# Query products of the late head pairs as 64x64 tiles in two banks

## Chip, cores and metric

The kernel runs on one core of a Trainium2 chip. The metric is the device time of one execution in microseconds (us), median of the runs. Engines: TensorE (PE; its weight loads are PEld), VectorE (DVE), ScalarE (ACT), GpSimd (POOL), and SyncE (SP), which issues most DMAs.

## What is computed

Linear attention with a norm, followed by a gated layer with spatial mixing:

```python
# batch 8, heads 8, seq 576, head_dim 64
kv  = einsum('bhsd,bhse->bhde', k, v)
out = einsum('bhsd,bhde->bhse', q, kv)
rms = sqrt(mean(out * out, axis=-1, keepdims=True) + 1e-06)
x   = (out / rms * g_norm)            # then to (batch, seq, 512)

h = maximum(x @ w_in, 0)              # 512 -> 1024
u, v = h[..., :512], h[..., 512:]
v_n = (v - mean(v)) / sqrt(var(v) + 1e-06)
v_s = einsum('ts,bsd->btd', w_spatial, v_n) + b_spatial[None, :, None]
result = (u * v_s) @ w_out            # 512 -> 512
```

## The kernel before

Heads are taken in pairs: pair p of batch b holds heads 2p and 2p+1, so a pair has 128 rows of head dimension. The sequence of 576 is four chunks of 128 and a tail of 64 rows, which is handled apart (`tail_a`, `tail_b`, `att_tail`). The large stages (`hv`, the u products, the spatial products, `out_unit`) split each f32 value into a high and a low fp32r part and use three products.

For batches 2 to 7 the attention of a batch is computed during the gated layer of the batch before. `att_four` (L172) forms the key-value products of all four pairs in two banks, copies their diagonal 64x64 blocks into `KVB` (a block for each pair, off-diagonal blocks zero), and then calls `att_two` (L207), which forms the query products of pairs 0 and 1 as 64x64 tiles: 32 calls, four to a slot of 64 rows by head and by half chunk, head 0 into one bank, head 1 into the other. Its matmuls are recorded on L181, those of a helper that queues each one behind the first. A call with f32 operands runs as two matmul instructions. `two_norm` (L219) takes the norm of one bank, that is of one head of both pairs: ScalarE squares the bank at once, VectorE sums it, `rsqrt` (ScalarE L272, VectorE L277 to L279) gives the factor, and VectorE multiplies it into one half of the columns of both `X2[0]` and `X2[1]`, strided.

Pairs 2 and 3 go through `att_q` one after the other: `att_qa` (L309) issues four 128x128 matmul calls against the whole block of `KVB` (L313) into one bank, then `norm_a` squares the bank in eight blocks of 64 with ScalarE's accumulator (L296), and `norm_b` (L305) multiplies the factor in. The result is one of `X2[0]` and `X2[1]`, in turn. `att_t` (L341) transposes a pair's result into a bank, and `split_x` (L334 ScalarE, L335 VectorE) writes the high and low part into `XH` and `XL`. All attention banks come from `ps_att`, three buffers in rotation.

The steps of a batch are put in a list by `att_steps` and are called where a letter `s` stands in the strings `FIRST`, `EVEN` and `ODD` (L53 to L66), between the products (`u`, `p`, `o`) of the running batch. For odd batches the late steps (T0, T1, Q2, Q3, T2, T3, then a copy of the tail) begin two products into the spatial stage (`p`); seven of its 14 products stand before Q2, one between Q3 and T2. For even batches three products stand before Q2, and five between Q2 and T2. The program order is a priority: the order on each engine is made when the program is built, from what is expected to be ready; `issue_after` alone keeps an instruction behind another on its engine. After each query product `issue` queues loads on SyncE: a query buffer is loaded again when its product has read it (`qt`, two buffers).

Of the kernel before, what the change touches and what calls it, by code (L numbers as in the profile page):

```python
# [8 lines left out]
F32 = mybir.dt.float32  # L9
# [3 lines left out]
AF = mybir.ActivationFunctionType  # L13
ALU = mybir.AluOpType
AX = mybir.AxisListType

B, H, S, D = 8, 8, 576, 64
DM, FF = 512, 1024
FH = FF // 2
P = 128  # L20
# [53 lines left out]
def body(ctx: ExitStack, tc, qT, kvm, kvt, g2, w_in, wsT, bsp, w_out, out):  # L74
    nc = tc.nc
# [11 lines left out]
    def persistent(shape, dt, name):  # L87
        return const.tile(shape, dt, name=name, tag=name)
# [29 lines left out]
    KVB = persistent([P, NP, P], F32, "KVB")  # L118
# [4 lines left out]
    ident = persistent([P, P], F32, "ident")  # L123
    gcol = persistent([P, 16], F32, "gcol")[:, 0:1]
    SUM = {n: persistent([P, 2, HS], F32, f"SUM{n}") for n in ("p1", "u2", "u3", "g")}
    n_gate, n_x, X2 = [0], [0], []
    edge = ctx.enter_context(tc.tile_pool(name="edge", bufs=1, side="right"))
    epsc = edge.tile([P, 8], F32, name="epsc", tag="epsc")[:, 0:1]

# [3 lines left out]
    keys, queries = {}, {}  # L133
# [70 lines left out]
        issue()  # L204
        issue()

    def att_two(b, st, matmul):  # L207

        qts = [queries.pop((b, i)) for i in range(2)]
        st["two"] = [ps_att.tile([P, 512], F32, name="pso", tag="att") for _ in range(2)]  # L210
        for c in range(NC):
            for j in range(2):
                for half in (0, D):
                    for h in (0, D):
                        at, t = (j * NC + c) * D, c * P + half
                        matmul(st["two"][h // D][half:half + D, at:at + D], qts[j][h:h + D, t:t + D],
                               st[j][h:h + D, h:h + D], start=True, stop=True)

    def two_norm(st, h):  # L219
        ps = st["two"][h]  # L220
        x = X2[2].rearrange("p j (c g e) -> p (j c) g e", g=2, e=D)[:, :, h]
        ss = small.tile([P, 8], F32, name="ss", tag="ss")
        nc.scalar.activation(x, heads(ps), AF.Square)
        nc.vector.tensor_reduce(ss, x, axis=AX.X, op=ALU.add)
        r = rsqrt(ss, 8, P, 1.0 / D, "h")
        nc.vector.tensor_tensor(x, heads(ps), r.unsqueeze(2).broadcast_to([P, 8, D]), op=ALU.mult)
        st[h] = X2[h]

    def att_k(b, pairs, st, copy=nc.vector.tensor_copy):
        ps = ps_att.tile([P, 512], F32, name="pskv", tag="att")  # L230
        to = KVB
        ends, first = [], None

        def product(p, of, h, c):
            at = (p - pairs[0]) * P + h
            return nc.tensor.matmul(ps[h:h + D, at:at + D], of[:, 0, h:h + D], of[:, 1, h:h + D],  # L236
                                    start=c == 0, stop=c == NC)

        for p in reversed(pairs):
            kv, kt, qs = keys.pop((b, p))  # L240
            for c in range(NC + 1):
                of = kv[:, :, c] if c < NC else kt
                for h in (0, D):
                    if first is None:
                        first = product(p, of, h, c).ins
                    else:
                        with tc.high_priority(), tc.issue_after(first):
                            product(p, of, h, c)
            st[p] = to[:, p]
            ends.append((p, qs))  # L250
        both = ps[:, 0:len(pairs) * P].rearrange("p (j e) -> p j e", e=P)
        own = slice(p, p + len(pairs))
        copy(to[0:D, own, 0:D], both[0:D, :, 0:D])
        nc.scalar.copy(to[D:P, own, D:P], both[D:P, :, D:P])  # L254
        for p, qs in reversed(ends):
            if qs is not None:
                att_end(p, st, qs)
        issue()
# [7 lines left out]
    def rsqrt(ss, n, rows, mul, tag):  # L266

        return rsqrt_b(*rsqrt_a(ss, n, rows, mul, tag))

    def rsqrt_a(ss, n, rows, mul, tag):  # L270
        y, r = (small.tile([P, n], F32, name=f"{x}{tag}", tag=f"{x}{tag}")[0:rows] for x in "yr")
        nc.scalar.activation(y, ss, AF.Abs_reciprocal_sqrt, bias=epsc[0:rows], scale=mul)  # L272
        return ss, y, r, mul
# [8 lines left out]
    def heads(ap):  # L282
        return ap.rearrange("p (h e) -> p h e", e=D)

    def norm_a(ps, rows=P, accumulate=False, soon=False):
        n = ps.shape[1] // D
        if soon:
            x = work.tile([P, 512], F32, name="xt", tag="stg", bufs=2)[:, 0:n * D]
        else:
            x = (X2[n_x[0] % 2] if X2 else pool_x.tile([P, 512], F32, name="x", tag="x"))[0:rows, 0:n * D]  # L290
            n_x[0] += 1
        ss = small.tile([P, 8], F32, name="ss", tag="ss")[0:rows, 0:n]
        if accumulate:
            for h in range(n):
                cols = slice(h * D, (h + 1) * D)
                nc.scalar.activation(x[:, cols], ps[0:rows, cols], AF.Square,  # L296
                                     accum_out=ss[:, h:h + 1])
        else:
            nc.scalar.activation(x, ps[0:rows], AF.Square)
            nc.vector.tensor_reduce(ss, heads(x), axis=AX.X, op=ALU.add)  # L300
        return ps, x, rows, rsqrt_a(ss, n, rows, 1.0 / D, "h")
# [21 lines left out]
    def att_q(b, p, st):  # L323
        att_qa(b, p, st, b > 1 and True)
        att_qb(b, p, st)

    def tail_a(b, st, accumulate=False, soon=False):
        st["xt"] = norm_a(st["tail"], P, accumulate, soon)

    def tail_b(b, st):  # L330
        st["xt"] = norm_b(*st["xt"])
# [5 lines left out]
    def att_t(b, p, st):  # L337
        x = st[p]
        ps = ps_att.tile([P, 512], F32, name="pstr", tag="att")
        for c in range(NC):  # L340
            nc.tensor.transpose(ps[:, c * P:(c + 1) * P], x[:, c * P:(c + 1) * P], ident)  # L341
        hi, lo = (X0H, X0L) if b == 0 else (XH, XL)
        split_x(ps, hi[:, p, 0:NT], lo[:, p, 0:NT])

    def att_tail(b, st):
        x = st["xt"]
        ps = ps_att.tile([P, 512], F32, name="pstt", tag="att")
        for p in range(NP if b < 2 else 2):
            nc.tensor.transpose(ps[:, p * P:(p + 1) * P], x[:, p * P:(p + 1) * P], ident)
        cols = slice(TAILC[b % 2], TAILC[b % 2] + TAIL)  # L350
        hi, lo = (X0H, X0L) if b < 2 else (XH, XL)
        n, i = (P, P - TAIL) if b < 2 else (TAIL, 0)
        v = ps[:, 0:NP * n].rearrange("q (p t) -> q p t", t=n)[:, :, i:n]
        split_x(v, hi[:, :, cols], lo[:, :, cols])
        if b == 1:
            own = slice(TAILC[0], TAILC[0] + TAIL)
            for to, of in (XH, hi), (XL, lo):
                nc.gpsimd.dma_start(f32(to[:, :, own]), f32(of[:, :, cols]))
# [7 lines left out]
    def att_steps(b):  # L366

        st = states.setdefault(b, {})

        def t2():  # L370
            att_t(b, 2, st)
            tail_a(b, st)
            tail_b(b, st)

        def tail():
            tail_a(b, st)
            tail_b(b, st)

        K = [lambda p=p: att_k(b, (p, p + 1), st) for p in (0, 2)]
        Q = [lambda p=p: att_q(b, p, st) for p in range(NP)]  # L380
        T = [lambda p=p: att_t(b, p, st) for p in range(NP)]
        end = lambda: att_tail(b, st)
        if b > 1:
            N = [lambda h=h: two_norm(st, h) for h in range(2)]
            late = [T[0], T[1], Q[2], Q[3], T[2], T[3]]
            if b % 2 == 0:
                return [*[K[0], lambda: att_four(b, st)] * (b == 2), *N, *late[:4], t2, T[3], end], []
            return [*N, lambda: (tail_a(b, st, soon=True), tail_b(b, st)), end], [*late, move_tail]
        if b % 2 == 0:
            return [*K[:1], Q[0], Q[1], T[0], *K[1:], Q[2], T[1], Q[3], t2, T[3], end], []  # L390
        return K + [tail, end], [Q[0], Q[1], T[0], Q[2], T[1], Q[3], T[2], T[3], move_tail]
# [360 lines left out]
    pool_x = opening.enter_context(tc.tile_pool(name="x", bufs=2))  # L752
# [120 lines left out]
    def room(b, p, kind):  # L873
        if kind == "q":
            return sum((x == 0) <= (y < 2) for x, y in queries) < 2
        return in_u(b, p) or sum(not in_u(*x) for x in keys) < 2

    def issue():

        while wanted[0] and todo and room(*todo[0]):  # L880
            wanted[0] -= 1
            att_load(*todo.pop(0))
# [47 lines left out]
    def enqueue(b, late=0):  # L930
        if b < NB:
            queue.extend(att_steps(b)[late])
# [55 lines left out]
    st = [states.setdefault(b, {}) for b in range(2)]  # L988
# [135 lines left out]
```

## Time and profile before

| | us |
|---|---|
| span of the profiled execution | 491.9 |
| three timed runs | 492.62, 495.11, 495.78 |
| their median | 495.11 |
| TensorE busy, VectorE busy, ScalarE busy | 482.5, 383.5, 276.4 |

The span goes from the first to the last instruction of the one profiled execution; the time of that execution beyond its span isn't listed, and the runs are 0.7 to 3.9 us above it. Busy times are shares of the span. In a timeline a row is one or more like instructions in a run, with the start of the first, and the time to the end of the last; as matmuls overlap, a row's slot is the time to the start of the next row.

### The profile page before, as it was taken

To read this page: it belongs to the slowest core of one execution; us is meant where nothing else is said; L and a number is where in the kernel's file an instruction comes from. 1 tells how busy PE (TensorE), PEld (TensorE's weight loads), DVE (VectorE), ACT (ScalarE), POOL (GpSimd) and SP (SyncE) were. 2 spreads that over 40 slices of the span, in tenths; PEclk is the share of its full clock that TensorE was granted. 3 is DMA by queue.
4 is the path that set the end of the run, shared out by engine and by line. 5 is a ranking of instruction groups with operands and counts; after the bars stand their busy time and mean duration, and the time that the engine had idled before them with its cause. 6 is when DMAs were issued, how large, how long until landed. Compare 5 with 4: busy or idle time off the path is not lost.

```text
span 491.9 us, 10170 instructions
## 1 busy us (share of the span) xinstructions
PE 482.5 (98%) x3796; PEld 434.9 (88%) x3796; DVE 383.5 (78%) x1029; ACT 276.4 (56%) x818; POOL 35.9 (7%) x71
## 2 busy tenths in 40 slices
PE   6999999999999999999999999999999999999996
PEld 6879999998978899889997899979998889989995
DVE  1889997884986797877986798977887779877770
ACT  3799845876425783368424694257733678246322
POOL 5001100000121010010000000010000101010000
PEclk9999999999999999999999999999999999999999
DMA  8999333553377036471536426372324702333413
GB/s 258 365 278 328 78 113 115 179 178 121 97 262 227 27 82 261 138 228 45 190 126 189 151 68 218 116 209 100 104 113 139 225 1 61 144 94 121 135 39 107
DMA packets 30357, 74.13 MB, mean 151 GB/s; under 512 B 6786, under 2 KB 9858, under 8 KB 28772
## 3 DMA queue, kind: packets, MB, share of 16 engines
q1 hardware_dynamic: 24852, 47.61, 30.1%
q0 software_dynamic: 5456, 25.87, 16.0%
q8 instruction: 30, 0.49, 0.4%
q14 instruction: 19, 0.16, 0.1%
HBM read 58.09 MB, written 13.11 MB: 145 GB/s over the span
## 4 chain that ended last, share of the span: by engine, by line
PE 90%; DMA 3%; DVE 3%; ACT 1%; SPq 1%; issue 0%; DVEq 0%
PE pso L398 21%; PE psh L431 17%; PE psb L638 7%; PE psub L638 6%; PE psa L638 6%; PE psc L638 5%; PE psuc L638 4%; PE psua L638 4%; PE pso L313 4%; PE pskv L181 3%; PE psu L398 3%; PE pstr L341 3%; PE psh L398 2%; DMA stage<-w_out 2%; PE pso L181 1%; PE pskv L236 1%
## 5 line engine op out<-in xcount | busy, mean ns | idle before, releaser
L398 PE MATMUL pso<-WO,G 128*128 128x512 f32 x384 | 95.6, 395 | 0.0
L398 PEld LDWEIGHTS pso<-WO,G 128*128 128x128 f32 x384 | 70.5, 188 | 15.2 <-issue 0.9
L434 ACT CAST G<-SUMg 128x288 fp32r<-128x288 f32 (+1 forms) x56 | 22.2, 405 | 62.0 <-DVE SUMg L660 62.0
L740 ACT COPY o<-pso 128x512 f32<-128x512 f32 x35 | 19.8, 588 | 52.8 <-PE pso L398 44.4
L435 DVE TENSOR_TENSOR VL<-v,VH 128x512 fp32r<-128x512 f32 (+1 forms) x60 | 36.4, 615 | 11.0 <-ACT VH L434 10.6
L431 PE MATMUL psh<-WVH,XH 128*128 128x512 f32 x112 | 43.8, 391 | 0.0
L431 PE MATMUL psh<-WVH,XL 128*128 128x512 f32 x112 | 43.7, 391 | 0.0
L431 PE MATMUL psh<-WVL,XH 128*128 128x512 f32 x112 | 43.6, 389 | 0.0
L434 ACT CAST VH<-v 128x512 fp32r<-128x512 f32 (+1 forms) x60 | 32.8, 563 | 11.6 <-DVE v L463 10.9
L418 ACT ACTIVATE v<-v,mv,rv 128x512 f32<-128x512 f32 x28 | 22.8, 813 | 7.8 <-DVE mv L417 6.1
L410 DVE BATCH_NORM_STATS2 s<-v 128x6 f32<-128x512 f32 x32 | 22.1, 692 | 5.4 <-ACT v L404 4.8
L431 PEld LDWEIGHTS psh<-WVH,XL 128*128 128x128 f32 x112 | 21.0, 188 | 4.6
L638 PE MATMUL psb<-WSH,VH 128*128 128x288 f32 x84 | 25.1, 300 | 0.0
L435 DVE TENSOR_TENSOR G<-SUMg,G 128x288 fp32r<-128x288 f32 (+1 forms) x56 | 23.4, 420 | 2.1
L431 PEld LDWEIGHTS psh<-WVL,XH 128*128 128x128 f32 x112 | 21.0, 188 | 4.4
L431 PEld LDWEIGHTS psh<-WVH,XH 128*128 128x128 f32 x112 | 21.0, 188 | 4.3
L638 PE MATMUL psb<-WSL,VH 128*128 128x288 f32 x84 | 24.7, 295 | 0.0
L638 PE MATMUL psb<-WSH,VL 128*128 128x288 f32 x84 | 24.1, 294 | 0.0
L404 ACT ACTIVATE v<-psh 128x512 f32<-128x512 f32 x32 | 19.1, 597 | 6.8 <-PE psh L431 5.8
L313 PE MATMUL pso<-KVB,qt 128*128 128x128 f32 x144 | 20.8, 293 | 1.8 <-DMA qt<-qT 1.3
L313 PEld LDWEIGHTS pso<-KVB,qt 128*128 128x128 f32 x144 | 19.5, 206 | 2.6 <-ACT KVB L254 2.2
L334 ACT ACTIVATE XH<-pstr,gcol 128x512 fp32r<-128x512 f32 x28 | 18.7, 688 | 5.3 <-PE pstr L341 5.3
(281 smaller groups left out, 1417.8 us busy)
## 6 DMA issues: line engine op xcount, KB each, us to landing
WO<-spare_o POOLq DMA_DIRECT2D x12, 1024.0 KB, 6.5
KV<-kvm SPq DMA_DIRECT2D x19, 512.0 KB, 5.5
UX<-spare_u POOLq DMA_DIRECT2D x18, 512.0 KB, 5.7
out<-o SPq DMA_DIRECT2D x32, 256.0 KB, 2.3
qt<-qT SPq DMA_DIRECT2D x28, 256.0 KB, 3.7
U<-kvm SPq DMA_DIRECT2D x12, 512.0 KB, 4.0
stage<-w_in SPq DMA_DIRECT2D x8, 512.0 KB, 7.5
KT<-kvt SPq DMA_DIRECT2D x32, 64.0 KB, 4.8
```

Of the source, the lines that this page charges most:

```text
L181: first[0] = nc.tensor.matmul(*args, **kw).ins
L313: nc.tensor.matmul(ps[:, c * P:(c + 1) * P], qt[:, c * P:(c + 1) * P], st[p], start=True, stop=True)
L334: nc.scalar.activation(hi, ps, AF.Copy, scale=gcol)
L398: nc.tensor.matmul(ps, lt, rh, start=i == 0, stop=i == n - 1)
L404: nc.scalar.activation(v, ps, AF.Relu)
L410: nc.vector.bn_stats(s6, v)
L418: nc.scalar.activation(v, v, AF.Identity, bias=m, scale=r)
L431: nc.tensor.matmul(ps, lt, rh, start=k == 0 and i == 0, stop=k == NP - 1 and i == 2)
L434: nc.scalar.copy(hi, x)
L435: nc.vector.tensor_tensor(lo, x, f32(hi), op=ALU.subtract)
L638: nc.tensor.matmul(ps, lt, rh, start=start and i == 0, stop=stop and i == len(pairs) - 1, skip_group_check=True)
L740: nc.scalar.copy(o, ps)
```

## The change

Pairs 2 and 3 of batches 2 to 7 go through `att_two` and `two_norm` as well. One step, `late_two`, issues 32 calls of 64x64 for both pairs, the first queued behind the last TensorE instruction traced, each further one behind the one before it, and then the two load steps; the norm of head 0 is part of that step, that of head 1 is the next. Their squares stay in blocks of 64 with ScalarE's accumulator. Each norm fills half of the columns of both `X2[0]` and `X2[1]`. The norm of an even batch's tail uses `X2[0]` as before.

```diff
-    n_gate, n_x, X2 = [0], [0], []
+    n_gate, X2 = [0], []
...
-    def att_two(b, st, matmul):
-
-        qts = [queries.pop((b, i)) for i in range(2)]
+    def att_two(b, st, matmul, first=0):
+
+        qts = [queries.pop((b, first + i)) for i in range(2)]
...
-                               st[j][h:h + D, h:h + D], start=True, stop=True)
-
-    def two_norm(st, h):
+                               KVB[h:h + D, first + j, h:h + D], start=True, stop=True)
+
+    def two_norm(st, h, first=0):
...
-        nc.scalar.activation(x, heads(ps), AF.Square)
-        nc.vector.tensor_reduce(ss, x, axis=AX.X, op=ALU.add)
+        if first:
+            for k in range(8):
+                nc.scalar.activation(x[:, k], ps[:, k * D:(k + 1) * D], AF.Square,
+                                     accum_out=ss[:, k:k + 1])
+        else:
+            nc.scalar.activation(x, heads(ps), AF.Square)
+            nc.vector.tensor_reduce(ss, x, axis=AX.X, op=ALU.add)
...
-        st[h] = X2[h]
+        st[first + h] = X2[h]
+
+    def last_pe():
+        return next(i for i in reversed(nc.cur_bb.bb.instructions) if i.engine == mybir.EngineType.PE)
+
+    def late_two(b, st):
+        row = [None]
+
+        def matmul(*args, **kw):
+            if row[0] is None:
+                with tc.issue_after(last_pe()):
+                    row[0] = nc.tensor.matmul(*args, **kw).ins
+                return
+            with tc.high_priority(), tc.issue_after(row[0]):
+                row[0] = nc.tensor.matmul(*args, **kw).ins
+
+        att_two(b, st, matmul, 2)
+        issue()
+        issue()
...
-            x = (X2[n_x[0] % 2] if X2 else pool_x.tile([P, 512], F32, name="x", tag="x"))[0:rows, 0:n * D]
-            n_x[0] += 1
+            x = (X2[0] if X2 else pool_x.tile([P, 512], F32, name="x", tag="x"))[0:rows, 0:n * D]
...
-            late = [T[0], T[1], Q[2], Q[3], T[2], T[3]]
+            late = [T[0], T[1], lambda: (late_two(b, st), two_norm(st, 0, 2)),
+                    lambda: two_norm(st, 1, 2), T[2], T[3]]
```

## Rows read from the trace of the kernel before

**Rows 1.** The page: span, and busy time of TensorE

```profile
span 491.9 us, 10170 instructions
...
PE 482.5 (98%) x3796; PEld 434.9 (88%) x3796; DVE 383.5 (78%) x1029; ACT 276.4 (56%) x818; POOL 35.9 (7%) x71
```

**Rows 2.** Waits of TensorE: us in total, times, longest us

```profile
PE pskv L236 <- DMA KV<-kvm: 1.7, 2, 1.4
PE pso L313 <- DMA qt<-qT: 1.3, 1, 1.3
...
```

**Rows 3.** The line of the late pairs' squares: duration min/median/max, first and last start

```profile
L296 ACT ACTIVATE xx<-pso x96: 201/250/376, 116.3 to 410.9; 128x64 f32<-128x64 f32 x96
```

**Rows 4.** Timeline of TensorE, batch 2, pairs 2 and 3 (start us, us)

```profile
115.17 1.06 PE L313 MATMUL pso<-KVB,qt 128*128 128x128 f32 x8
115.99 3.01 PE L398 MATMUL pso<-WO,G 128*128 128x512 f32 x12
118.83 1.06 PE L313 MATMUL pso<-KVB,qt 128*128 128x128 f32 x8
```

**Rows 5.** The same timeline: nine output matmuls among spatial ones

```profile
134.76 2.23 PE L398 MATMUL pso<-WO,G 128*128 128x512 f32 x9
136.83 0.29 PE L638 MATMUL psc<-WSH,VH 128*128 128x288 f32 x1
```

**Rows 6.** The same timeline: tiled products of batch 3, pairs 0 and 1

```profile
143.25 0.63 PE L398 MATMUL pso<-WO,G 128*128 128x512 f32 x2
143.81 0.69 PE L181 MATMUL pskv<-U 128*64 128x64 f32 x16
...
144.54 0.50 PE L398 MATMUL pso<-WO,G 128*128 128x512 f32 x1
144.88 1.76 PE L398 MATMUL pso<-WO,GT 128*128 128x512 f32 x7
...
148.23 1.16 PE L181 MATMUL pso<-KVB,qt 64*64 64x64 f32 x64
149.32 0.66 PE L181 MATMUL pst<-KVB,QS 128*64 128x128 f32 x8
```

**Rows 7.** Timeline of TensorE: end of batch 2's u products, transposes, spatial stage

```profile
176.20 0.95 PE L638 MATMUL psuc<-T,UX 128*128 128x288 f32 x6
176.99 0.96 PE L638 MATMUL psub<-T,UX 128*128 128x288 f32 x6
177.96 0.40 PE L638 MATMUL psub<-UX,WUH 128*128 128x288 f32 x1
178.20 0.29 PE L638 MATMUL psub<-T,WUH 128*128 128x288 f32 x1
...
179.65 0.60 PE L341 MATMUL pstr<-ident,xx 128*128 128x128 f32 x4
...
180.88 0.30 PE L638 MATMUL psa<-WSH,VH 128*128 128x288 f32 x1
```

**Rows 8.** Windows: length, then busy PE, PEld, DVE, ACT, POOL, clock, DMA

```profile
170.40:181.00 10.60, 10.59 (x82) 10.32 (x81) 9.62 (x35) 9.63 (x46) 1.07 (x2) 1.00 0.33 87
181.00:196.00 15.00, 15.00 (x144) 14.77 (x143) 12.11 (x31) 5.85 (x15) 1.11 (x2) 1.00 0.61 220
```

**Rows 9.** Timeline of ScalarE: first square and last read of batch 3's pair 2

```profile
171.52 0.22 ACT L296 ACTIVATE xx<-pso 128x64 f32<-128x64 f32 x1
...
173.01 0.25 ACT L296 ACTIVATION_READ_ACCUMULATOR xx<-pso 128x1 f32 x1
```

**Rows 10.** Timeline of SyncE: the two query loads after batch 3's late products

```profile
171.51 4.42 SPq L166 DMA_DIRECT2D qt<-qT  x2
```

**Rows 11.** The page, DMA issues: KB each, median us from issue to landing

```profile
qt<-qT SPq DMA_DIRECT2D x28, 256.0 KB, 3.7
```

**Rows 12.** Timeline of TensorE: batch 3's T0 and T1

```profile
159.74 1.04 PE L341 MATMUL pstr<-ident,xx 128*128 128x128 f32 x8
```

**Rows 13.** Timeline of VectorE: the scaled result of batch 3's pair 2

```profile
178.45 0.68 DVE L305 TENSOR_TENSOR xx<-pso,rh 128x512 f32<-128x512 f32 x1
```

## Prediction

> **What bounds the kernel now.** I read the page first, then who waited for whom on TensorE, then the timeline of TensorE around the touched products. The page [rows 1] has TensorE busy for 482.5 of 491.9 us. Busy can hide a wait, because pipelined matmuls overlap, so I looked at the waits: the two largest of TensorE are 1.7 and 1.3 us [rows 2] and concern loads of the opening. From the second batch on, TensorE issues one matmul behind another, and the time is the sum of their slots (start to next start), of the changes between kinds of matmul, and of little else. So the change is priced by the slots that it takes from TensorE and gives to it; what it does on the other engines counts only if TensorE comes to wait.
>
> **What is removed.** For pairs 2 and 3 of batches 2 to 7 there are 12 products; the squares of their norms stand as 96 blocks, 8 to a pair [rows 3]. Each product is four calls that run as 8 matmuls of 128x128. In batch 2 the first starts at 115.17 and what follows at 115.99, that is 0.82 us [rows 4]. The 12 matmuls that follow reach to 118.83, 2.84 us, where nine of that kind take 2.07 us elsewhere [rows 5], 0.230 each, or 2.76 for 12. So leaving the f32 product costs another 0.08. One pair costs 0.90 us, two cost 1.80 us a batch, six batches 10.8 us. Entering costs nothing that I can see.
>
> **What is added.** The trace already has the new form: pairs 0 and 1 of the same batches run as 64 matmuls of 64x64 into two banks, from 148.23 to 149.32, 1.09 us [rows 6]. This holds the work and the drains inside it. There the neighbours are other tiled products; the new block will stand among 128x128 ones, so an entry and an exit come on top. The nearest rows are the 20 tiled matmuls between output products: before them two matmuls take from 143.25 to 143.81, 0.56 where 0.46 is the pace, so the entry costs 0.10; behind them one takes 0.34 instead of 0.23, so the exit costs 0.11 [rows 5, 6]. The new block costs 1.09 + 0.10 + 0.11 = 1.30 us.
>
> **A rule weighed.** The rows put 0.21 us on the two changes of tiling, beside the drains already inside the 1.09 [rows 6]. The Trainium skill, TensorEngine Tiling, section Tiling Modes (Key Properties), says that a change of tiling mode, other than a change of tile, drains the engine; it gives no figure, and the trace agrees. Without any outer drain the gain would be 6 x (1.80 - 1.09) = 4.3 us, with them it is 6 x (1.80 - 1.30) = 3.0 us; I take the second.
>
> **The sum on TensorE.** 6 x 0.50 = 3.0 us less. Bounds: 4.3 us if each new block stands beside other f32 products, which then share the drains. On the other side, something may be placed inside the block: a visit of 128x128 matmuls costs an exit and an entry again, 0.21 outside, and about 0.15 inside (the 20 tiled matmuls take 0.73 where ten pairs at 0.058, an estimate from the pace inside that row, take 0.58), 0.36 together. One such cut in each batch leaves 6 x 0.14 = 0.8 us.
>
> **What moves.** The first of the new matmuls is queued behind the last TensorE instruction traced. In an odd batch's work this is the seventh product of the spatial stage, where the old products stood before that stage began (it begins at 180.88 [rows 7]; they ran from about 170 on). With it move 16 square blocks on ScalarE (count and width unchanged: 8 a pair before, 8 a bank now), two reciprocal roots, and eight VectorE instructions. They leave a stretch where VectorE is busy 9.62 and ScalarE 9.63 of 10.60 us for one with 12.11 and 5.85 of 15.00 [rows 8]. The moved work is about 3.5 us of ScalarE (two times 1.74, from 171.52 to the end of the last read at 173.26 [rows 9]) and some 2 us of VectorE, part of which lies in the second stretch already; both fit. I cost the move at nothing: TensorE's own products hide it. If that cover failed, the price is that of the third case below. The strided rather than contiguous writes of the squares and the scaled result cost nothing, as pairs 0 and 1 use the same layout now.
>
> Two query loads are also issued behind the block, together instead of one after each pair. Now they are issued from 171.51 on [rows 10] and land 3.7 us after issue [rows 11]. Behind the block in an odd batch there are still seven products of at least six matmuls at 0.13 and some 40 output matmuls at 0.23 before the next batch's early products read them, 5.5 + 9.2 = 14.7 us. Queued behind these loads on SyncE are the key loads of the next batch, wanted at the same late time. GpSimd's queue is not passed. So nothing is late there.
>
> The second of the two banks is the one that the first transpose (T0) filled; the old second product needed it as well, later than the first. T0 in batch 3 runs at 159.74 [rows 12], the new block after 180.88, so I cost this wait at nothing. If the block came too early, every instruction behind its second matmul would stand on TensorE until the split of T0 ends.
>
> One stall may go. In batch 3, six matmuls take 0.79 us (176.20 to 176.99), the next six 0.97, and one more 0.24 instead of 0.13 [rows 7], some 0.28 us in all, just where the second norm fills ScalarE and VectorE. If it comes from there it goes in three odd batches, 0.85 us; if not, nothing. I take nothing.
>
> **Rivals.** (a) Forecast: 3.0 us less by slots alone. The profiled span of 491.9 becomes 488.9. The median of the runs shown, 495.11, is 3.2 us above the profiled span (the lowest only 0.7 above), and I take the difference off the median: 492.1 us.
>
> (b) The block is cut up: other matmuls are placed between its first and its last. One cut in each batch leaves 0.8 us, 494.3 us; two make 6 x (0.50 - 0.72), 1.3 us slower, 496.4. For it: only order on TensorE is asked for, not closeness. Against: the 64 matmuls of pairs 0 and 1, traced the same way, stand in one piece [rows 6]. It is also the way in which the change does not do what it says.
>
> (c) Slower: the transposes of pair 2 wait. Before, T2 needed the norm of pair 2 alone, and T2 started 0.52 us after its result (178.45 + 0.68 = 179.13, T2 at 179.65 [rows 7, 13]). Now each head's norm fills half of both pairs, so T2 needs both norms: 2 x 1.74 of squares, 0.68 for the last product and about 0.8 for the small steps between (an estimate, from the three small and one root instruction that surround it), 5.0 us from the end of the block. In batches 3, 5 and 7 the program has just one product of the spatial stage in between, 8 x 0.13 = 1.1 us; if T2 keeps that place, TensorE stands 3.9 us in each, 11.8 us, and the time is 492.1 + 11.8 = 503.9 us. It decides against the change from 1.0 us of stall in each of these three batches. In batches 2, 4 and 6 there are over 5 us between. Against it: the order on TensorE is not that of the program: T0 of batch 3, which the program has behind two products of that stage, runs 21 us before them [rows 7, 12], so transposes are put where their operands are expected to be ready, and no wait of TensorE for a norm is among the largest [rows 2].
> The Trainium skill, TensorEngine Tiling, section Performance Considerations (PSUM Bottleneck), says that after such a speedup the emptying of PSUM may become what binds. By it this case would be the likely one; the rows so far show other work in that cover for pairs 0 and 1, and I give it the chance below.
>
> (d) Faster by more: the blocks share drains (4.3 us) and the stall of 0.28 us goes in three batches (0.85 us): 5.1 us, 490.0 us. For it: ScalarE and VectorE are relieved where both are over 90% busy [rows 8]. Against: all six blocks would have to find such neighbours.
>
> **How the numbers follow.** Chances: (a) 0.62, (b) 0.17, (c) 0.11, (d) 0.10. A measurement of this kernel tells about 1%, 5 us, from no change. (d) lies at that line and is counted as faster, and (a) comes out beyond it by its own scatter (the three runs span 3.2 us) with some 0.06: faster 0.16. (c) is slower: 0.11. The rest, 0.73, is within 1%. The range goes from 1.5 us under (d) to just over two cuts of (b), 488.5 to 497.0; (c) stays outside it.
>
> **What would show it.** Right: twelve pieces of 64 matmuls of 64x64 where there were six, each new one about 1.1 us with 0.1 more on either side; no product of 128x128 with KVB left after batch 1; waits of TensorE as small as now; the span 3 us shorter. A step is wrong if a new block starts late on a bank, if it is in several pieces, if T2 or T3 starts behind a wait for the second norm, or if the slots of the output and spatial products differ. The prediction falls if the span changes by under 1 or over 5 us.

## The result, and the profile after

The changed kernel takes 499.08 us (median of seven runs, 496.45 to 500.60) where the kernel before, in as many runs, takes 495.11 (492.62 to 496.20). The ratio is 1.0092 with a 95% interval from 1.0069 to 1.0115: 0.9% slower, some 4.5 us, where 3.0 us less were forecast; the time lies outside the range. Of the 6.0 us between the two profiled spans, 2.2 arose before 97 us, where both kernels run the same instructions in the same order. That opening varies from one execution to the next: its 701st matmul comes 96.1 us behind the first one after, 93.9 before, and 94.0 in the profiles of the first two experiments below. So 3.7 us remain to be explained.

The head of the page after, beside [rows 1]:

```profile
span 497.9 us, 10746 instructions
...
PE 480.0 (96%) x4084; PEld 430.3 (86%) x4084; DVE 384.3 (77%) x1029; ACT 276.2 (55%) x818; POOL 35.8 (7%) x71
```

TensorE is busy for 2.5 us less, which is nearly the 3.0 us that the slots promised. The span is longer all the same, so TensorE now waits. The waits of TensorE after, beside [rows 2] (us in total, times, longest us):

```profile
PE psub L661 <- DVE U L633: 3.3, 3, 1.1
PE psub L661 <- ACT v L427: 1.9, 2, 0.9
PE pso L335 <- DMA qt<-qT: 1.4, 1, 1.4
...
PE psub L661 <- ACT U L619: 0.6, 1, 0.6
```

The two at the head are new. They are u products (psua, psub and psuc are their banks, psa to psc those of the spatial stage), which the change doesn't touch: three wait for VectorE's addition to U, two for ScalarE's relu that empties a bank (L427). The one of 0.6 us, also new, is a u product of the last batch. The wait for a query load in the opening, 1.3 us before, is 1.4.

The new block itself, on TensorE's timeline after (batch 3, pairs 2 and 3; start us, us):

```profile
186.10 0.29 PE L669 MATMUL psa<-WTL,TB 128*128 128x288 f32 x1
186.32 0.27 PE L243 MATMUL pso<-KVB,qt 64*64 64x64 f32 x1
186.33 0.28 PE L246 MATMUL pso<-KVB,qt 64*64 64x64 f32 x3
186.43 0.22 PE L243 MATMUL pso<-KVB,qt 64*64 64x64 f32 x1
186.43 1.05 PE L246 MATMUL pso<-KVB,qt 64*64 64x64 f32 x59
187.41 0.40 PE L661 MATMUL psb<-WSH,VH 128*128 128x288 f32 x1
187.65 0.30 PE L661 MATMUL psb<-WSL,VH 128*128 128x288 f32 x1
```

All 64 matmuls stand in one piece, 1.09 us from 186.32 to 187.41. The slot ahead of them is 0.22 and that behind 0.24 where 0.13 is the pace, so 0.09 and 0.11 on top: 1.29 us, the 1.30 of the forecast.

What became of the time of the old products? In an odd batch's attention they stood in the u stage, at 170.43 and 174.51 in batch 3. After, the same stretch on TensorE:

```profile
175.61 1.75 PE L661 MATMUL psub<-T,UX 128*128 128x288 f32 x12
178.47 0.40 PE L661 MATMUL psub<-UX,WUH 128*128 128x288 f32 x1 [1.11 <-DVE U L633]
```

and on VectorE:

```profile
175.55 1.40 DVE L504 TENSOR_TENSOR TA<-v,TA 64x512 fp32r<-64x512 f32 x2
176.98 0.87 DVE L504 TENSOR_TENSOR TA<-SUMg,TA 64x256 fp32r<-64x256 f32 x2
177.88 0.16 DVE L300 SCALAR_TENSOR_TENSOR rv<-yv 128x1 f32<-128x1 f32 x1
177.96 0.81 DVE L633 TENSOR_TENSOR U<-psub,U 128x288 f32<-128x288 f32 x2
```

Twelve matmuls from 175.61 at 0.13 each are issued by 177.2. The product behind them goes on in the same bank, so it must wait until VectorE has read it (L633), and on VectorE the low part of the tail's v (L504, 2.3 us) stands ahead of that. Before, TensorE came to this place 0.18 us early [rows 7], with VectorE's addition (L610 there) at

```profile
177.46 0.45 DVE L610 TENSOR_TENSOR U<-psub,U 128x288 f32<-128x288 f32 x1
```

Counted from the start of the stage, that is 18.7 us before and 18.0 after: without the norms VectorE is 0.7 us sooner, but TensorE, without the two products, is 1.8 us sooner. So now it comes 1.3 us early.

In an even batch's attention the cover can be seen directly. Before, on TensorE's timeline (batch 4):

```profile
227.44 0.43 PE L638 MATMUL psua<-XH,WUL 128*128 128x288 f32 x2
227.70 1.50 PE L313 MATMUL pso<-KVB,qt 128*128 128x128 f32 x12
228.96 0.51 PE L638 MATMUL psub<-T,WUH 128*128 128x288 f32 x2
```

and after:

```profile
229.28 0.29 PE L661 MATMUL psua<-XH,WUL 128*128 128x288 f32 x1
230.50 0.53 PE L661 MATMUL psub<-T,WUH 128*128 128x288 f32 x2 [0.93 <-ACT v L427]
```

The reason is on ScalarE's timeline after:

```profile
228.97 0.69 ACT L356 ACTIVATE XH<-pstr,gcol 128x512 fp32r<-128x512 f32 x1
229.55 0.40 ACT L457 CAST VH<-v 128x256 fp32r<-128x256 f32 x1
229.85 0.60 ACT L427 ACTIVATE v<-psh 128x512 f32<-128x512 f32 x1
```

ScalarE empties the bank that the product needs (L427) behind seven other pieces of work that follow one another from 226.36. Before, it did so at

```profile
227.68 0.61 ACT L404 ACTIVATE v<-psh 128x512 f32<-128x512 f32 x1
```

That is 5.3 us from the start of the stage, as after: ScalarE's date hasn't moved. Before, the 12 old matmuls filled 1.26 us while ScalarE got there. Without them TensorE stands.

By stages the loss closes. The u stage (first psua to first psa) lost 1.8 us of old products in each of the five in which the attention of batches 3 to 7 is made, yet is only 0.34 to 0.40 us shorter in the three for odd batches (22.15 became 21.79 for batch 3) and 0.59 in the two for even ones (13.78 became 13.19): 2.3 us in all. The rest of the cycle, where the block now stands, is 1.31, 1.29, 0.77, 1.31 and 1.37 us longer: 6.05. For odd batches a transpose also left the u stage and six matmuls of another product came into it, so there the split between the two is rough; for even batches nothing of TensorE's work moved but the products. Batch 2, where both forms stand among output products, gained 1.0 us (52.74 became 51.71 from the first output product of all to the first of these u stages), and the last batch's u stage lost 0.9. 6.05 - 2.3 - 1.0 + 0.9 = 3.7.

The squares cost about what they did, a median of 269 ns where it was 250 [rows 3]:

```profile
L225 ACT ACTIVATE xx<-pso x96: 214/269/337, 118.7 to 425.9; 128x64 f32<-128x64 f32 x96
```

### The profile page after: what moved, and what is told of

The parts are those of the page before. It is cut to its first block, busy times and chain, and to the rows that moved or that the text cites. A ratio compares the mean times of both kernels' runs of the same rounds, so it can differ in the third digit from the quotient of the medians.

```text
span 497.9 us, 10746 instructions
## 1 busy us (share of the span) xinstructions
PE 480.0 (96%) x4084; PEld 430.3 (86%) x4084; DVE 384.3 (77%) x1029; ACT 276.2 (55%) x818; POOL 35.8 (7%) x71
## 4 chain that ended last, share of the span: by engine, by line
PE 80%; DVE 7%; ACT 6%; DMA 5%; issue 1%; SPq 1%; ACTq 0%; DVEq 0%
PE pso L421 20%; PE psh L454 15%; PE psb L661 6%; PE psa L661 5%; PE psub L661 4%; PE psc L661 4%; PE psuc L661 3%; PE pskv L181 3%; PE psu L421 3%; PE psua L661 2%; PE pstr L363 2%; DMA stage<-w_out 2%; PE psh L421 2%; DVE TA L504 2%; PE pso L335 1%; PE pskv L259 1%
## 5 line engine op out<-in xcount | busy, mean ns | idle before, releaser
L421 PE MATMUL pso<-WO,G 128*128 128x512 f32 x384 | 94.5, 395 | 0.0
L356 ACT ACTIVATE XH<-pstr,gcol 128x512 fp32r<-128x512 f32 x28 | 18.8, 688 | 10.0 <-PE pstr L363 10.0
L225 ACT ACTIVATE xx<-pso 128x64 f32<-128x64 f32 x96 | 20.5, 269 | 5.3 <-PE pso L246 5.3
L427 ACT ACTIVATE v<-psh 128x512 f32<-128x512 f32 x32 | 19.1, 597 | 5.9 <-PE psh L454 5.3
L357 DVE SCALAR_TENSOR_TENSOR XL<-pstr,gcol,XH 128x512 fp32r<-128x512 f32 x28 | 20.7, 740 | 2.0 <-ACT XH L356 1.7
```

The costliest lines, as they stand in the source:

```text
L225: nc.scalar.activation(x[:, k], ps[:, k * D:(k + 1) * D], AF.Square, accum_out=ss[:, k:k + 1])
L356: nc.scalar.activation(hi, ps, AF.Copy, scale=gcol)
L357: nc.vector.scalar_tensor_tensor(lo, ps, gcol, f32(hi), op0=ALU.mult, op1=ALU.subtract)
L421: nc.tensor.matmul(ps, lt, rh, start=i == 0, stop=i == n - 1)
L427: nc.scalar.activation(v, ps, AF.Relu)
```

## The experiments

Theory A: the old products stood in time that TensorE would have waited anyway, so taking them out gave little, while the block is paid for whole where it stands now. Ratios are to the kernel before, with 95% intervals.

**The place without the tiles.** The kernel before, with its 128x128 late products queued where the new block stands:

```diff
...
-            late = [T[0], T[1], Q[2], Q[3], T[2], T[3]]
+            late = [T[0], T[1], lambda: (late_q(b, st), late_norm(2, st)), lambda: late_norm(3, st), T[2], T[3]]
```

> The kernel before with the one difference that the 128x128 products of pairs 2 and 3 are issued in one go, queued behind the last TensorE instruction traced, at the place where the changed kernel has its 64x64 block; norms pair by pair as before. Theory A (lost cover): the old products stood in the u stage just ahead of a product that waits for ScalarE or VectorE, and hid that wait; moved away they uncover it, whatever their shape. Then the u stage shows waits of 1.1 to 1.3 us here too, the products cost their full 1.8 us a batch in the spatial stage, and the time is about 3 us over the changed kernel, 1.011 to 1.017 of before. Rival B (the tiles, their drains and the norms across both pairs are what costs): the time is that of before, 0.997 to 1.003, and no such waits show.

Measured: 1.0138 (1.0115 to 1.0162). A holds: without a single new tile the kernel is slower, and its waits of TensorE have the same lengths at the same products:

```profile
PE psub L661 <- DVE U L633: 3.3, 3, 1.1
...
PE psub L661 <- ACT v L427: 1.9, 2, 0.9
```

The changed kernel differs from this one by the tiles, with norms by head instead of by pair, and is 0.0046 of 495 us, 2.3 us, better (by the two intervals, some 0.7 to 3.9). So the 3.0 us of the forecast were about right as the worth of the tiles at one place; the move took 6.8 us.

**Work put back as a filler.** The changed kernel, with four calls of the identity (8 matmuls, read by nobody) ahead of the product that waits, in the u stages of batches 2 to 7. (In odd batches' attention two products also change their order.)

```diff
...
+                k = 14 - len(u)
+                if b > 1 and k == (12 if b % 2 == 0 else 4):
+                    with tc.issue_after(fill(behind_u)):
+                        u.pop(0)()
...
```

> The changed kernel with four more f32 calls (8 matmuls of 128x128, about 0.9 us) in the u stage of batches 2 to 7, ahead of the product that waits; their result is read by nobody. TensorE gets 6 x 0.9 = 5.4 us more work. Theory A: they fit into the waits, the u stages keep their length within 0.3 us each, and the time is that of the changed kernel within 1.5 us (1.006 to 1.012 of before). Rival B: TensorE is the bound throughout, and the time is 5.4 us over the changed kernel, 1.018 to 1.022 of before.

Measured: 1.0060 (1.0042 to 1.0078): some 5 us of TensorE work more, and not slower than the changed kernel with 1.0092. The head of its page:

```profile
span 495.9 us, 10842 instructions
...
PE 484.7 (98%) x4132; PEld 435.5 (88%) x4132; DVE 384.5 (78%) x1029; ACT 276.6 (56%) x818; POOL 35.9 (7%) x71
```

and the first u wait in its list of TensorE's waits, 0.6 us in total where there were 3.3:

```profile
PE psub L672 <- DVE U L644: 0.6, 3, 0.2
```

TensorE is busy 4.7 us longer than after, and the time is no longer. The two u stages for even batches last 13.19 us with the filler as without it. That is what a hole in the schedule looks like: one can fill it for nothing.

**The block left free to float.** The changed kernel without the order on the block's first matmul:

```diff
-                with tc.issue_after(last_pe()):
-                    row[0] = nc.tensor.matmul(*args, **kw).ins
+                row[0] = nc.tensor.matmul(*args, **kw).ins
```

> The changed kernel without queuing the first of the 64 matmuls behind the last one traced; the block then goes where it is ready, in the u stage, with its first call cut off from the other 31. Theory A: the waits of over 1 us in the u stage are gone or below 0.4, and the time is 0.994 to 1.001 of before, the cut costing some 0.36 us a batch. Rival B: the time stays at that of the changed kernel, 1.007 to 1.011.

Measured: 1.0134 (1.0114 to 1.0154); both missed. In batches 3 to 7 the block is cut into 1 and 31 calls, as rival (b) had it (0.26 and 1.08 us where the whole takes 1.09), and floats back into the u stage. The odd batches lose their wait of over 1 us there, but a single new one of 2.1 us comes up in an even one:

```profile
PE psub L660 <- DVE U L632: 2.1, 1, 2.1
```

**The block pinned inside the u stage**, behind the ninth product (odd) or the fourth (even), first as it is, then with its norms queued behind ScalarE's work traced so far:

```diff
...
-                with tc.issue_after(last_pe()):
+                with tc.issue_after(behind_u.get(b) or last_pe()):
...
+                if 14 - len(u) == (9 if b % 2 == 0 else 4):
+                    behind_u[b + 1] = last_pe()
```

and for the second, beside these:

```diff
...
+        with tc.issue_after(act):
+            two_norm(st, h, 2)
...
-            late = [T[0], T[1], lambda: (late_two(b, st), two_norm(st, 0, 2)),
-                    lambda: two_norm(st, 1, 2), T[2], T[3]]
+            late = [T[0], T[1], lambda: (late_two(b, st), late_norm(b, st, 0)),
+                    lambda: late_norm(b, st, 1), T[2], T[3]]
```

> The changed kernel with the block of 64 queued behind a product of the u stage instead of behind one of the spatial stage: behind the ninth u product for odd batches, behind the fourth for even ones, so that it stands in one piece just ahead of the product that waits in the changed kernel. Theory A: the block takes the place of the waits and is mostly hidden; the u stage is at most 0.4 us longer than in the changed kernel, the rest of a batch 1.3 us shorter, and the time is 0.992 to 0.998 of before. Rival B: 1.006 to 1.011 of before, as in the changed kernel.

> The run with the block in the u stage, with the norms' ScalarE work held back: queued behind the last ScalarE instruction traced, so that it starts in the spatial stage. If that run lost its time because ScalarE had 16 blocks of squares ahead of the u stage's own work, and theory A is right on the block, the u stage is now no longer than in the changed kernel in every batch, and the time is 0.993 to 0.999 of before. If a block in the u stage is itself the trouble, it stays above 1.015.

Measured: 1.0219 (1.0184 to 1.0253) and 1.0181 (1.0122 to 1.0239); A's numbers missed. In the first, two u stages are 6.7 and 4.2 us longer than before. In the first of the two, TensorE stands for VectorE:

```profile
351.20 1.76 PE L663 MATMUL psub<-T,UX 128*128 128x288 f32 x6 [2.31 <-DVE U L626]
```

VectorE in turn has to wait, as ScalarE's timeline shows:

```profile
348.03 0.20 ACT L225 ACTIVATE xx<-pso 128x64 f32<-128x64 f32 x1
...
351.50 0.32 ACT L225 ACTIVATE xx<-pso 128x64 f32<-128x64 f32 x1
...
352.52 1.14 ACT L459 CAST VH<-v 128x512 fp32r<-128x512 f32 x2 [0.28 <-DVE v L488]
```

Most of the 16 squares, each with its read, stand ahead of the last two casts, for which VectorE's splits wait. TensorE had time to spare there; ScalarE has none when both norms come at once. Part of the 6.7 and 4.2 us is TensorE's clock: it fell as such waits ended, and the granted clock was 0.50 (1.2 GHz) from 351.3 to 358.1 us and from 402.5 to 405.9 us (the last section has what such a stretch costs). The second variant has other waits in other places, and such stretches as well; by the measure set for it, above 1.015, a block in the u stage is itself the trouble, and what in it isn't shown. So a block of both pairs is no equal of two products one after the other, even in the same stage.

**The squares.** The changed kernel, with each bank squared at once and summed by VectorE, as for pairs 0 and 1:

```diff
-        if first:
+        if False:
```

> The changed kernel with the late norms' squares taken as the early ones are: the whole bank at once on ScalarE, summed by VectorE. Theory A (the old products covered waits of the u stage): the norms have no part in the loss, and the time is that of the changed kernel, 1.006 to 1.012 of before. Rival C (two norms of eight blocks one behind the other hold up ScalarE and with it the gates of the spatial stage): ScalarE does 2 x 1.1 us less a batch, and the time falls by 2 to 4 us, to 1.001 to 1.005 of before.

Measured: 1.0127 (1.0058 to 1.0196), just above A's range; the interval is wide, but its lower end is above C's 1.005. C is out; the form of the squares isn't what costs.

**Another order of u products.** The last two of the 14 products of each u stage queued behind the eleventh, so that the waiting one comes later; for odd batches' attention alone, then for all (there with T0 and T1 of even batches held back too):

```diff
-                u.pop(0)()
+                k = 14 - len(u)
+                with tc.issue_after(after_p30) if b % 2 == 0 and k > 11 else ExitStack():
+                    u.pop(0)()
+                if k == 10:
+                    after_p30 = last_pe()
```

and for all, with `b > 1` in the condition, beside it:

```diff
...
+        with tc.issue_after(behind_u[b]) if b in behind_u and b % 2 == 0 and p < 2 else ExitStack():
+            att_t_(b, p, st)
...
```

> The changed kernel with one order asked for in the u stages in which an odd batch's attention is made: the last two u products, which wait for VectorE's reading of the bank they add to, are queued behind the two products that come before them in the program (those that the build had put after them). No work is added or taken away. Theory A: the wait of 1.3 us goes in three batches, 3 to 4 us, and the time is 1.000 to 1.004 of before. Rival B (TensorE is the bound, the tiles cost it): no change, 1.007 to 1.011.

> The same order asked for in all u stages from batch 2 on, and the transposes of pairs 0 and 1 of even batches queued behind the fourth u product, where the changed kernel's other wait of 1.1 us stands, so that they stand in it. Theory A: both kinds of wait go, 6 to 7 us less than the changed kernel, 0.993 to 0.999 of before: the saving of slots that was forecast then shows. Rival B: 1.006 to 1.011.

Measured: 1.0180 (1.0131 to 1.0229) and 1.0211 (1.0169 to 1.0252): both slower, both missed. The first wait in the first one's list:

```profile
PE psuc L661 <- DVE U L634: 6.7, 3, 2.2
```

and in the second's:

```profile
PE psuc L667 <- DVE U L640: 8.8, 6, 2.2
```

The wait for L633 is gone, but the product that took its place waits for the next addition on VectorE, twice as long. So with these two orders TensorE's order doesn't decide: VectorE's dates do. A part of both losses is again TensorE's clock (last section).

**VectorE's dates moved.** The changed kernel, with the subtractions of L504 on GpSimd; and, as a control, the same edit in the kernel before:

```diff
-                nc.vector.tensor_tensor(TA[i][other, cols], x[own], f32(hi), op=ALU.subtract)
+                nc.gpsimd.tensor_tensor(TA[i][other, cols], x[own], f32(hi), op=ALU.subtract)
```

> The changed kernel with the four subtractions that make the low part of the tail's v (2.3 us of VectorE in each u stage, ahead of the U addition for which TensorE waits 1.1 us) on GpSimd, which is idle there. Theory A2 (what bounds the u stage without the old products is VectorE's order, the addition behind these subtractions): the three waits of 1.1 us go, and the ratio to the kernel before is 1.001 to 1.005. Rival (the wait moves to another reader, as it did when the products were reordered): 1.007 to 1.012.

> The control to the run with the tail's subtractions on GpSimd: the same edit in the kernel before, where the old products stand in the u stage. Theory A2 (the edit helped the changed kernel because it took away waits that only the loss of the cover had opened; before, TensorE stands 0.2 us at that place): ratio to the kernel before 0.997 to 1.001. Rival (taking this work off VectorE is worth 2 to 3 us in any kernel, and the run showed nothing about the cover): 0.993 to 0.996.

Measured: 1.0038 (1.0015 to 1.0061), against 1.0092 without the edit: 2.7 us better (by the two intervals, some 1.1 to 4.3). The control: 0.9985 (0.9964 to 1.0006), 0.7 us better, within what can't be told from nothing. By the profiled executions, from the first of these u stages to the end, the edit gives 1.7 us in the changed kernel and 0.8 in the control. So a half to three quarters of the gain were found only where the old products are gone. The two u waits in the first one's list:

```profile
PE psub L661 <- ACT v L427: 1.9, 2, 0.9
...
PE psub L661 <- DVE U L633: 0.9, 3, 0.3
```

VectorE's wait falls from 3.3 to 0.9 us. VectorE's addition starts 17.5 us into the stage instead of 18.0, and each u stage for an odd batch is 0.5 us shorter. ScalarE's two waits, which the edit doesn't touch, stay and are a good part of what is still lost. That these go too when ScalarE empties the bank earlier wasn't tried.

In the control, TensorE's timeline where [rows 7] showed the stall of 0.18 us:

```profile
176.69 0.96 PE L638 MATMUL psub<-T,UX 128*128 128x288 f32 x6
177.48 0.60 PE L341 MATMUL pstr<-ident,xx 128*128 128x128 f32 x4
177.84 0.38 PE L638 MATMUL psub<-UX,WUH 128*128 128x288 f32 x1
```

Six matmuls take 0.79 us again, and the transpose of pair 2 has moved up: it now stands where the stall was. On VectorE the addition starts at

```profile
177.16 0.45 DVE L610 TENSOR_TENSOR U<-psub,U 128x288 f32<-128x288 f32 x1
```

That is 18.8 us into the stage, where it was 18.7 without the edit. So in the control the edit didn't bring VectorE's date forward, and what an earlier date is worth where the old products still stand isn't shown.

**The products left out**, old ones from the kernel before, block from the changed one:

```diff
...
+            for c in (0, 2 * P):
+                nc.tensor.matmul(ps[:, c:c + 2 * P], one[:, 0:P], one, start=True, stop=True)
...
```

> The kernel before, with the query products of pairs 2 and 3 of batches 2 to 7 left out: two short bf16 products of constants write each of their banks instead, so that ScalarE and VectorE have the same norms to do on other numbers (the attention of those pairs isn't computed). By an estimate from slots of 0.23 us for 512 columns, the four short ones cost 0.46 us a batch where the old ones cost 1.80: 1.34 us less on TensorE in each of six batches, 8.0 us. Theory A (in the u stage the old products stood in time that TensorE would have waited anyway): only batch 2 gains it whole, the five others some 0.4 us each as in the changed kernel, 3.3 us in all, ratio to the kernel before 0.990 to 0.997. Rival B (TensorE's slots bound the u stage): 8.0 us, 0.982 to 0.986.

> The changed kernel with its new block left out in the same way: four short bf16 products of constants, queued at the block's place, write its two banks (the attention of pairs 2 and 3 isn't computed). 1.30 - 0.46 = 0.84 us less on TensorE a batch, 5.0 us in six. Theory A (at its new place the block is paid for whole): ratio to the kernel before 0.996 to 1.003. Rival D (what the change costs hangs on the late norms and their effects, and not on the block's slots): stays at 1.007 to 1.011.

Measured: 1.0208 (1.0162 to 1.0253, from two executions) and 1.0232 (1.0196 to 1.0268): with less work, both are slower than every theory had them. They don't price the products. With shorter products the program came out in another order, and the waits changed place, as in the second:

```profile
PE psub L666 <- ACT v L432: 4.5, 2, 3.6
PE psh L459 <- ACT o L768: 3.0, 2, 2.8
```

How much of the loss is the order, how much the other dates of the norms, and how much the clock isn't shown: behind such waits the granted clock in the second was 0.51 from 232.4 to 235.8 us and 0.50 from 341.7 to 345.1 us. What a new order alone can cost is better read from the two runs above that asked for nothing else, 1.0180 and 1.0211 against 1.0092: 4 to 6 us.

**What can be kept.** The block in batch 2 alone, and that together with the subtractions on GpSimd:

```diff
...
+            if b > 2:
+                late = [T[0], T[1], Q[2], Q[3], T[2], T[3]]
```

> The kernel before with the new block in batch 2 alone, where its place among output products is that of the old ones; batches 3 to 7 keep their 128x128 products. Theory A: this batch gains what the slots say, 0.5 to 1 us, and nothing else moves: ratio 0.997 to 1.000. Rival B (the tiled block itself costs more than its slots): 1.001 or more.

> The new block in batch 2 alone, and the tail's subtractions on GpSimd: the two edits that cost nothing so far, put together. Theory A: 0.5 to 1 us from batch 2 and up to 0.5 us from the waits of 0.2 us in three u stages: ratio 0.995 to 0.999. Rival (each edit has the program ordered anew, and the gains of single edits don't add): 1.000 or more.

Measured: 0.9982 (0.9962 to 1.0001) and 0.9955 (0.9931 to 0.9979). The first can't be told from nothing by its interval. The second beats both kernels, 493.05 us against 494.23 beside it in medians, and 2.2 us by the ratio. The head of its page:

```profile
span 488.9 us, 10282 instructions
...
PE 479.2 (98%) x3844; PEld 432.0 (88%) x3844; DVE 381.5 (78%) x1013; ACT 276.1 (56%) x818; POOL 52.1 (11%) x87
```

None of its u products is among the larger waits of TensorE.

## Why the prediction was wrong

*What is removed, what is added:* right as slots. The block is 1.09 with 0.09 and 0.11 beside it, against a forecast of 1.30 in all; TensorE's busy time fell by 2.5 us; and the tiles are worth 2.3 us where both forms stand at one place. In batch 2, where both forms stand among output products, the 0.5 us came, and as much again, which the slots don't explain (other products change places there too).

*What moves:* this is the step that failed, in the words "I cost the move at nothing: TensorE's own products hide it". Measured alone, in the first experiment, the move costs 6.8 us. TensorE's products do hide the norms behind the new place. The question not asked was what the old products had hidden at the old one. TensorE's busy time, 482.5 of 491.9 us, was read as a sum of slots ("the time is the sum of their slots"), so that every slot taken out is time gained. But in the u stage two other engines were nearly as late as TensorE: VectorE's addition behind the tail's splits, and ScalarE's relu behind its casts. Of 1.8 us removed in a batch, some 0.5 became time in the five batches where the products had stood there, and the rest of the cycle, with the block's 1.3 in it, grew by 1.2 on average: the block was paid nearly whole. The windows had shown it [rows 8]: 9.62 and 9.63 of 10.60 us busy on VectorE and ScalarE in just the stretch that the work left. They were read as relief for these two, not as the bound that remains when TensorE is relieved. The prediction did price a lost cover, but that of the new place, by T2.

*One stall may go:* the sign was wrong. The 0.28 us [rows 7] was put down to the second norm. Its 0.18 us at the waiting product were the tip of the wait for VectorE: when the old products left, this grew to 1.3 us, though VectorE was 0.7 us sooner without the norms. A stall of a fifth of a microsecond was here the sign that another engine is right behind.

*Loads, banks, strided writes:* nothing late, as forecast. No wait of TensorE for a query load other than the 1.4 us in the opening, and none for T0's bank.

*Rivals:* (b) didn't come in the changed kernel, but did once the block's first matmul was free. (c) had the right sign and the wrong place: the one wait of a transpose in the list is in the opening. A better rival was in the rows: in the u stage VectorE and ScalarE are right behind TensorE, and the move gives 0.5 of 1.8 us there and costs 1.3 us in five batches.

The Trainium skill, TensorEngine Tiling (Array Packing), section Performance Considerations, warns under PSUM Bottleneck that tiling speeds up TensorE and not the emptying of PSUM, which may then bind. The trace agrees in part: both new waits are for a bank to be read, 1.1 and 0.9 us. But they are banks of the u stage, not of the tiles, and the same two waits appear with no tile in the late products at all (the first experiment).

Open is how much of the even batches' part would go with an earlier relu. Open in part is why the u stage of the last batch, in which no attention is made and which so lost no cover, grew by 0.9 us: 0.6 of it is TensorE's wait for ScalarE's relu L619, which now stands behind a cast and a normalization. The first experiment has this wait too (0.9 us); the run with whole-bank squares has none, and its stage is as short as before (11.12 us). What put ScalarE's work in that order isn't shown.

## What to carry to other kernels

Before work is moved off an engine, ask what it covers where it stands: compare the dates at which the other engines deliver there with the date at which the bound engine will now arrive, and price the slot at the new place whole. The stage in which VectorE and ScalarE were over 90% busy gave back 0.5 of the 1.8 us taken from TensorE. And where a program is ordered at build time, test a single edit with a control, and look in the control's trace whether the edit did there what it did in the other kernel: the new order alone, with the fall of the clock behind its waits, was worth 4 to 6 us here.

## What the runs showed of the hardware

A wait of TensorE can cost more than its length, because its clock can fall. In the first run with another order of u products, TensorE stands 2.2 us in each of three u stages, ahead of the same product. In the second of the three the granted clock fell near the end of the wait; the timeline, and the window from there (columns as in [rows 8]):

```profile
296.69 0.61 PE L661 MATMUL psuc<-XH,UX 128*128 128x288 f32 x1 [2.25 <-DVE U L634]
...
296.60:300.00 3.40, 3.31 (x14) 3.31 (x15) 1.11 (x6) 1.69 (x3) 0.00 (x0) 0.51 0.00 0
```

There the clock is at the lower of its two levels, 1.2 GHz, and slots are 0.24 us where 0.13 is the pace. This stage lasts 24.40 us, the other two 23.04 and 22.96: the stretch cost 1.4 us. The changed kernel has none between 19 us and its last microsecond. Of the runs that came out slower, both with the block in the u stage, both with another order and the one without the block have one or two such stretches behind their waits.

A subtraction on GpSimd holds up VectorE. With the subtractions there, GpSimd's timeline:

```profile
172.89 2.63 POOL L504 TENSOR_TENSOR TA<-v,TA 64x512 fp32r<-64x512 f32 x2 [18.15 <-ACT TA L503]
```

and VectorE's beside it:

```profile
173.03 1.15 DVE L440 SCALAR_TENSOR_TENSOR mv<-mv,rv 128x1 f32<-128x1 f32 x1
...
174.59 0.95 DVE L300 SCALAR_TENSOR_TENSOR rv<-yv 128x1 f32<-128x1 f32 x1
175.46 0.45 DVE L633 TENSOR_TENSOR U<-psub,U 128x288 f32<-128x288 f32 x1
```

Two subtractions that took 1.40 us on VectorE take 2.63 on GpSimd, and in that time VectorE's steps of one column take 0.95 and 1.15 us, where 0.13 to 0.16 is usual. Additions that read a bank (L633, 0.45) are as fast as ever. The Trainium skill, GPSIMD Engine Reference, section Specifications, says that the two share their SBUF interfaces and contend where VectorE has two inputs in SBUF; these rows agree, and put some 0.8 to 1.0 us on one such meeting. It still paid, because what was moved stood in front of the addition that TensorE waited for.
